# A new order for the first block's products, a narrow idle stream of zeros, and zeroing moved to GpSimd

## The chip, the cores and the metric

The kernel runs on one core of a Trainium2 chip. A core has five engines, each with its own queue of instructions: TensorE (PE in the profile; its weight loads are PEld), VectorE (DVE), ScalarE (ACT), GpSimd (POOL) and SyncE (SP, which here only issues transfers). Engines wait for one another by semaphores, and each engine runs its own instructions in the order in which they were written. The metric is the device time of one execution in microseconds (us); lower is better.

## The reference

Two stages follow each other. The first is a linear attention with decay, for 4 sequences (b), 8 heads (h), 768 steps (t) and 64 elements per head; the second is a feed-forward layer on the 3072 tokens, of width 512 and hidden width 2048.

```python
gamma = 1.0 - 2.0 ** (-5.0 - np.arange(H))
for t in range(S):
    state = gamma[None, :, None, None] * state + np.einsum('bhd,bhe->bhde', k[:, :, t], v[:, :, t])
    y[:, :, t] = scale * np.einsum('bhd,bhde->bhe', q[:, :, t], state)
...
h = np.maximum(x @ w_in, 0.0)          # x: y as 3072 x 512
return h * h @ w_out
```

## The kernel before

**Chunks and blocks.** Each sequence is cut into 6 chunks of 128 steps, 24 chunks in all. Within a chunk the attention is computed with matrices: scores of every key against every query, masked, times the values (`scores`, `outputs`); what earlier chunks contribute goes through a 64 x 64 state per head (`state`). The decay is put into scale factors of q and k (`scale_q`, `scale_kv`). q and k are turned on TensorE (`transpose_q`, `transpose_k`), and ScalarE copies the turned tiles out: `qT` at L414, `k_bd` at L428 in two halves. `outputs` leaves the chunk in a bank that ScalarE copies to `xt` (L531). Chunks 0 to 3 are done in pairs by `..._pair` functions, chunks 4 to 7 by `attend`, and later ones by `attend2`. The feed-forward layer works on blocks of chunks: block 0 has four chunks (512 tokens), the others two.

**The front.** Before the first block there is no feed-forward work. The code loads q, k, v and the first quarter of `w_in` (SP's queue), scales, turns and multiplies for chunks 0 to 3, and between these products it lets TensorE run idle products, `keep_awake(n)` (L359): n products of 128 x 512 with the identity matrix `ident`, whose result nobody reads. `ident` is made by GpSimd (L237, L238). `cast_pair_v` casts the values of a pair to bf16, on GpSimd or with `on_scalar` on ScalarE.

**Block 0.** `ffn_pieces(0)` is a generator; each `yield` ends a piece. Pieces 4 to 15 compute one 128-row slice each of `x @ w_in` (L848) with `relu` (L857) and a squaring on VectorE (L828). Then `second_products` multiplies by `w_out`. Two of its four chunks are done plainly (`plain(j)`, two row blocks of `w_out` each, L1039). The other two are done with seven instead of eight block products, which needs sums and differences of blocks: of `w_out` (`sum_w_out`: `t1` to `t4` in the tiles `w_sum`, L336, on VectorE) and of the hidden values (`s1` to `s4`, L1002, on VectorE). `product(...)` (L1006) multiplies them into four half-bank results `pa`, `pb`, `pd`, `pe`; several of them are started with the first half of the products (`lo`) and ended with the second (`hi`). ScalarE copies the first part of `pa` to `a` (L1063) before further products are added onto `pa`. `w_out` comes in four quarters by `load_w_out(g)` on GpSimd's queue (L185); `plain(2g)` and `plain(2g+1)` use quarter g, the second half of the sums uses quarters 2 and 3.

**The hand-written schedule.** `put(place, what, ...)` puts an action before the piece with that number. Before each piece `before(n)` runs the actions of place n in the order in which they were put, and then the squarings (`take_squares`). So one list of places sets the order of every engine's queue. The numbers for chunk 4 before the change are: `scale_q` at 13 and 15, `scale_kv` at 18, `transpose_q` 19, `transpose_k` 21, `scores` 23 and 25, `state` 25, `outputs` 29; for chunk 5: `scale_kv` 25, `transpose_k` 28, `scores` 30 and 32, `outputs` 34. In block 0 the pieces after place 16 are: `plain(0)` to `plain(3)` (places 16 to 19), first halves of `pd` and `pb` (20), `plain(4)`, `plain(5)` (21, 22), first half of `pe` (23), `plain(6)`, `plain(7)` (24, 25), `pa` (26), `pd` (27), `pb` (28), `pe` (29), and the two halves of `s3` times `t3` onto `pb` (30, 31). Block 1 begins at place 32.

Some tiles that stand beside blocks have off-diagonal halves that must be zero; `zero_off_diagonal` (L375) writes them on VectorE at places 35 to 44.

Of the kernel before, what the change touches and what calls it, by code (L numbers as in the profile page):

```python
# [9 lines left out]
FP32 = mybir.dt.float32  # L10
BF16 = mybir.dt.bfloat16
I32 = mybir.dt.int32

AF = mybir.ActivationFunctionType
ALU = mybir.AluOpType
# [16 lines left out]
def kernel(  # L32
# [9 lines left out]
    nc = tc.nc  # L42
    P = nc.NUM_PARTITIONS
# [152 lines left out]
        load_w_in(g)  # L196


    lng = const.tile([P, H], FP32)
    for h in range(H):  # L200
        nc.gpsimd.memset(lng[:, h : h + 1], float(np.log(gammas[h])))
# [125 lines left out]
    HN = DM // 2  # L327
    sums = [const.tile([P, NFB // 2, HN], BF16, name=f"w_sum{i}") for i in range(4)]

    def sum_w_out(half):  # L330

        src = w_out_halves[half].rearrange("s (j k) (n c) -> s k n j c", k=2, n=2)
        (b11, b12), (b21, b22) = ([src[:, k, n] for n in range(2)] for k in range(2))
        t1, t2, t3, t4 = (t[:, 4 * half : 4 * half + 4] for t in sums)
        for out, in0, in1 in ((t1, b12, b11), (t2, b22, t1), (t3, b22, b12), (t4, b21, t2)):
            yield nc.vector.tensor_tensor(out=out, in0=in0, in1=in1, op=ALU.subtract)  # L336

    def cast_w(kind, g, halves=(0, 1), on="VVSG"):

# [11 lines left out]

    idle_ps = []

    def keep_awake(n, width=4 * C, pool=ps_f, name="psf"):
        if not idle_ps:
            idle_ps.append(pool.tile([P, 4, P], FP32, name=name))
        wide = max(1, width // C)
        for _ in range(n):
            nc.tensor.matmul(  # L359
                idle_ps[0][:, 0:wide, 0 : width // wide],  # L360
                lhsT=ident[:],
                rhs=ident[:, None, 0 : width // wide].to_broadcast([P, wide, width // wide]),
                start=True,
                stop=True,
            )

    def end_awake():
        idle_ps.clear()
# [3 lines left out]
    xts = {}  # L372

    def zero_off_diagonal(t, hh):
        nc.vector.memset(t[halves[hh], :, 1 - hh, :], 0.0)  # L375

    def scale(engine, out, by, table):
        engine.tensor_tensor(  # L378
# [204 lines left out]
    def cast_pair_v(m, r, on_scalar=False):  # L583
        at[m]["v"] = pair_view(v_bd2s[m // 2])
        if on_scalar:
            nc.scalar.activation(at[m]["v"][:, r], raw_v[m][:, r], AF.Copy)
        else:
            nc.gpsimd.tensor_copy(at[m]["v"][:, r], raw_v[m][:, r])
# [392 lines left out]
    def last_of_first():  # L981

        def halves_of(k, c):
            return [
                t.rearrange("e (j k) (c t) -> e k c j t", k=2, c=4)[:, k, 2 + c] for t in h2s[0]
            ]

        (a11, a12), (a21, a22) = ([halves_of(k, c) for k in range(2)] for c in range(2))
        n = NFB // 4
        s1, s2, s4 = (  # L990
            [
                t.rearrange("e (x j t) -> e x j t", x=2, t=C)[:, x]
                for x in range(2)
            ]
            for t in (spare[:, i * HN * 4 : (i + 1) * HN * 4] for i in range(3))
        )
        s3 = a21
        b = lambda k, c: lambda j: w_out_bf[j // 2][:, 2 * (j % 2) + k, c * HN : (c + 1) * HN]
        t1, t2, t3, t4 = (lambda j, t=t: t[:, j] for t in sums)

        def add(out, in0, in1, op=ALU.add):
            nc.vector.tensor_tensor(out=out, in0=in0, in1=in1, op=op)  # L1002

        def product(to, left, right, js, start=True, stop=True):
            for j in js:
                nc.tensor.matmul(  # L1006
                    to,
                    lhsT=left[j // n][:, j % n],
                    rhs=right(j),
                    start=(start and j == 0),  # L1010
                    stop=(stop and j == NFB // 2 - 1),
                    skip_group_check=True,
                )

        def first_sums(x):
            add(s1[x], a21[x], a22[x])
            add(s2[x], s1[x], a11[x], ALU.subtract)

        def last_sums():
            for x in range(2):  # L1020
                add(s3[x], a11[x], a21[x], ALU.subtract)
            for x in range(2):
                add(s4[x], a12[x], s2[x], ALU.subtract)

        def second_products():
            ops = [ps_f.tile([P, DM], FP32, name="psf") for _ in range(2)]
            pa, pe, pd, pb = (
                t[:, n * HN : (n + 1) * HN]
                for t in [ps_f.tile([P, DM], FP32, name="psf") for _ in range(2)]
                for n in range(2)  # L1030
            )
            oa, ob = (opool.tile([P, DM], FP32, name="osb") for _ in range(2))
            a, u, v = (upool.tile([P, HN], FP32, name=f"u{i}") for i in range(3))
            r0 = 2 * C

            def plain(j):
                for f in (2 * j, 2 * j + 1):
                    for c, op in enumerate(ops):
                        nc.tensor.matmul(  # L1039
                            op[:],  # L1040
                            lhsT=h_of(0, f)[:, 0, c * C : (c + 1) * C],
                            rhs=w_out_bf[f // FPQ][:, f % FPQ, :],
                            start=(f == 0),
                            stop=(f == NFB - 1),
                        )
                product(pa, a11, b(0, 0), (j,))

            lo, hi = range(0, 4), range(4, 8)
            for j in range(4):
                plain(j)  # L1050
                yield
            product(pd, s1, t1, lo)
            product(pb, s2, t2, lo, False)
            yield
            for j in range(4, 6):
                plain(j)
                yield
            product(pe, a22, t4, lo, False)
            yield
            plain(6)  # L1060
            yield
            plain(7)
            nc.scalar.activation(a[:], pa, AF.Copy)  # L1063
            for c, op in enumerate(ops):
                osb = opool.tile([P, DM], FP32, name="osb")
                nc.scalar.activation(osb[:], op[:], AF.Copy)
                nc.sync.dma_start(out[c * C : (c + 1) * C], osb[:])
            yield
            product(pa, a12, b(1, 0), lo, False)
            product(pa, a12, b(1, 0), hi, False)  # L1070
            nc.scalar.activation(oa[:, 0:HN], pa, AF.Copy)
            yield
            product(pd, s1, t1, hi)
            yield
            product(pb, s2, t2, hi)
            add(u[:], pb, a[:])
            yield
            product(pe, a22, t4, hi)
            yield
            product(pb, s3, t3, lo, False)  # L1080
            yield
            product(pb, s3, t3, hi, False)
            add(v[:], pb, a[:])
            add(ob[:, HN:DM], pd, v[:])
            add(ob[:, 0:HN], pe, v[:])

            def last_product():
                product(pd, s4, b(1, 1), range(8), False)
                add(oa[:, HN:DM], pd, u[:])
                yield  # L1090
                nc.sync.dma_start(out[r0 + C : r0 + 2 * C], ob[:])
                yield
                nc.sync.dma_start(out[r0 : r0 + C], oa[:])
                yield

            kept.append(last_product())
            yield

        return first_sums, last_sums, second_products

    open_ps = {}

# [15 lines left out]
    def ffn_pieces(tb):  # L1118
        nch = BLOCKS[tb]
        TB = nch * C  # L1120
        if tb == 0:
            first_sums, last_sums, second_products = last_of_first()
            put(11, first_sums, 0)
            put(17, first_sums, 1)
            put(22, last_sums)
            for f in range(FPQ, NFB):
                hp = ps_f.tile([P, TB], FP32, name="psf")
                first_product(tb, hp[:], f, slice(0, TB))
# [70 lines left out]
    def small_pt():  # L1199
        return ptpool.tile([P, NPAIR, 2, C], BF16, name="pt").rearrange("s p hh t -> s (p hh t)")  # L1200

    spare = hpool.tile([P, 4096], BF16, name="h2")
    keep_awake(7, pool=ps_y, name="y")
    scale_q4(0, 0)
    scale_q4(0, 1)
    transpose_q4(0, 0, *tp)
# [39 lines left out]
    state_pair(0, 1, "SV")  # L1246
    cast_w("in", 0, (0,), "GGGG")
    cast_pair_v(2, 0)
    cast_pair_v(2, 1)
    first_unit(0, 0, 0, (0,))  # L1250
    first_unit(0, 0, 1, (0,))
    cast_w("in", 0, (1,), "GGVV")
# [21 lines left out]
    def put(place, what, *args):  # L1274
        parts.setdefault(place, []).append((what, args))
# [4 lines left out]
    def attend(m, scaled, places):  # L1280
        if m % 2 == 0:
            put(scaled, scale_q, m, 0)
            put(scaled + 2 if m == 4 else scaled, scale_q, m, 1)
            put(places[0], transpose_q, m)
        put(18 if m == 4 else places[0], scale_kv, m)
        put(places[1], transpose_k, m)
        put(places[2], scores, m, 0)
        put(places[3], scores, m, 1)
        put(places[3], state, m)
        put(places[4], outputs, m)  # L1290
# [20 lines left out]
    for m, which, place in ((6, "k", 16), (6, "v", 17), (7, "k", 18), (7, "v", 19)):  # L1311
        put(place, load_kv, m, which)
    put(10, cast_w, "in", 3)
    for half, at_places in enumerate(((20, 20, 20, 20), (24, 24, 26, 26))):
        made = sum_w_out(half)
        for place in at_places:
            put(place, next, made)
    attend(4, 13, (19, 21, 23, 25, 29))
    attend(5, None, (25, 28, 30, 32, 34))
    attend(6, 31, (33, 35, 37, 39, 42))  # L1320
    attend(7, None, (38, 42, 44, 46, 49))
    packed = pack_constants()
    put(27, next, packed)
# [76 lines left out]
```

## Time and profile before

| What | Value |
|---|---|
| median of 3 runs | 204.95 us (204.93 to 205.1) |
| the profiled execution's own time | 205.18 us |
| its span in the trace | 203.0 us |
| busy share of the span: PE, PEld, DVE, ACT, POOL | 96%, 80%, 74%, 63%, 37% |
| chain that ended last: share on PE | 93% |
| data read from and written to memory, mean rate | 27.26 MB and 6.29 MB, 165 GB/s |

All times inside the execution are counted from the start of the span. The profiled execution lies 0.23 us above the median, and 2.2 us of it lie outside the span. A busy PE includes the idle products of the front.

### The profile page before, as it was taken

How to read it: one execution, taken by the hardware profiler on the slowest of the kernel's cores; microseconds unless marked ns; L12 is line 12 of the kernel's file. 1: busy time of each engine (PE TensorE's matmuls, PEld its weight loads, DVE VectorE, ACT ScalarE, POOL GpSimd, SP SyncE). 2: the span in 40 equal slices, each digit the busy share in tenths (PEclk: the TensorE clock that was granted, in tenths of full speed). 3: DMA queues.
4: the chain of work that ended last, by engine and by line, in shares of the span. 5: the costliest groups of instructions: out<-in, count | busy, mean ns of one | idle time of the engine just before them, and what ended most of it. 6: DMA issues, size and time to landing. Idle time of an engine off the chain costs nothing.

```text
span 203.0 us, 5812 instructions
## 1 busy us (share of the span) xinstructions
PE 195.8 (96%) x2351; PEld 163.3 (80%) x2351; DVE 150.0 (74%) x322; ACT 127.5 (63%) x258; POOL 75.4 (37%) x143
## 2 busy tenths in 40 slices
PE   5989999999999999999999999999999999999993
PEld 1558545669975998999999999999899999999883
DVE  3786898898797679677787777777787787485374
ACT  8764873455744676693794784774785775763730
POOL 8683721087220873461722084323382022100000
PEclk9999999999999999999999999999999999999999
DMA  5999999999798798979999479999999856200202
GB/s 167 356 374 397 321 198 196 243 232 251 226 203 200 190 141 131 200 180 251 145 215 197 140 130 187 175 227 199 166 133 195 155 107 53 103 3 0 107 0 105
DMA packets 92250, 36.55 MB, mean 180 GB/s; under 512 B 68544, under 2 KB 88256, under 8 KB 92224
## 3 DMA queue, kind: packets, MB, share of 16 engines
q1 hardware_dynamic: 77312, 32.52, 67.8%
q0 software_dynamic: 14912, 3.67, 19.2%
q8 instruction: 18, 0.29, 0.6%
q14 instruction: 8, 0.07, 0.1%
HBM read 27.26 MB, written 6.29 MB: 165 GB/s over the span
## 4 chain that ended last, share of the span: by engine, by line
PE 93%; DVE 2%; DMA 2%; issue 1%; ACT 1%; DVEq 0%
PE psf L848 42%; PE psf L882 18%; PE tp L882 7%; PE psf L1039 3%; PE psf L1174 3%; PE psf L1006 3%; DMA qn<-in_q_dram 2%; PE y L805 2%; PE st L749 2%; PE y L798 2%; PE c_ps L776 2%; PE c_ps L644 1%; PE y L359 1%; PE y L523 1%; PE st L447 1%
## 5 line engine op out<-in xcount | busy, mean ns | idle before, releaser
L848 PE MATMUL psf<-xt,w_in_bf 128*128 128x256 bf16 (+2 forms) x880 | 92.3, 259 | 0.2 <-issue 0.2
L848 PEld LDWEIGHTS <-w_in_bf 128*128 128x128 bf16 x880 | 71.2, 98 | 11.4 <-issue 0.2
L857 ACT ACTIVATE h<-psf 128x512 bf16<-128x512 f32 x96 | 56.1, 595 | 21.3 <-PE psf L848 19.0
L828 DVE TENSOR_TENSOR h<-h 128x512 bf16<-128x512 bf16 x80 | 33.6, 432 | 21.6 <-ACT h L857 21.2
L727 POOL COPY v_bd<-v 64x512 bf16<-64x512 bf16 x32 | 21.6, 675 | 75.0 <-DVE v L719 70.9
L882 PEld LDWEIGHTS <-h 128*128 128x128 bf16 x288 | 26.5, 98 | 3.0 <-DVE h L828 0.3
L160 POOL DMA_DIRECT2D k_big<-in_k_dram x32 | 21.1, 675 | 0.0
L882 PE MATMUL psf<-w_sum,h 128*128 128x256 bf16 x136 | 19.1, 273 | 0.0
L882 PE MATMUL tp<-w_out_bf,h 128*128 128x256 bf16 x136 | 19.1, 273 | 0.0
L882 PE MATMUL psf<-w_sum,k_bd 128*128 128x256 bf16 x144 | 17.9, 273 | 0.0
L878 DVE TENSOR_TENSOR u<-psf,u 128x256 f32<-128x256 f32 x18 | 7.6, 424 | 11.2 <-PE psf L882 10.8
L882 PEld LDWEIGHTS <-k_bd 128*128 128x128 bf16 x144 | 13.8, 98 | 1.5
L785 ACT ACTIVATE s_bd<-c_ps 64x256 bf16<-64x256 f32 x29 | 10.7, 370 | 6.5 <-PE c_ps L776 6.5
L878 DVE TENSOR_TENSOR osb<-psf,u 128x256 f32<-128x256 f32 x26 | 10.3, 421 | 6.1 <-PE psf L882 5.8
L378 DVE TENSOR_TENSOR qs<-qn,qf 128x512 bf16<-128x512 f32 x20 | 14.2, 713 | 0.0
L786 ACT ACTIVATE s_bd<-c_ps 64x256 bf16<-64x256 f32 x29 | 11.0, 379 | 0.4
L756 DVE TENSOR_TENSOR pt<-st,cmask 128x512 bf16<-128x512 f32 x16 | 11.0, 688 | 0.1
L719 DVE TENSOR_TENSOR v<-stage,kf 128x512 bf16<-128x512 f32 x16 | 11.0, 685 | 0.0
L812 ACT ACTIVATE xt<-y 128x512 bf16<-128x512 f32 x16 | 9.6, 599 | 1.8 <-PE y L805 1.2
L918 ACT ACTIVATE osb<-tp 128x256 f32<-128x256 f32 x8 | 3.1, 385 | 12.2 <-PE tp L882 12.2
L826 ACT ACTIVATE h<-h 128x512 bf16<-128x512 bf16 x16 | 10.1, 630 | 0.5
L878 DVE TENSOR_TENSOR k_bd<-h 128x512 bf16<-128x512 bf16 x18 | 10.1, 559 | 0.3
(149 smaller groups left out, 296.1 us busy)
## 6 DMA issues: line engine op xcount, KB each, us to landing
qn<-in_q_dram SPq DMA_DIRECT2D x12, 512.0 KB, 5.5
out_dram<-osb SPq DMA_DIRECT2D x23, 256.0 KB, 2.6
stage<-in_v_dram SPq DMA_DIRECT2D x32, 96.0 KB, 4.1
stage<-in_moe_w_in_dram SPq DMA_DIRECT2D x4, 512.0 KB, 7.2
stage<-in_moe_w_in_dram SPq DMA_DIRECT2D x2, 1024.0 KB, 8.4
w_out_bf<-in_moe_w_out_dram POOLq DMA_DIRECT2D x4, 512.0 KB, 10.1
kn<-in_k_dram SPq DMA_DIRECT2D x6, 256.0 KB, 6.3
k_big<-in_k_dram POOLq DMA_DIRECT2D x32, 48.0 KB, 3.8
```

The costliest lines, as they stand in the source:

```text
L160: nc.gpsimd.dma_start(t[rows, :, p, hh, :], k[b, 2 * p + hh, (i + 3 * n) * C : (i + 3 * n + 3) * C].rearrange("(w s) d -> s w d", s=64),)
L378: engine.tensor_tensor(out=out, in0=by, in1=table[:, :, None].to_broadcast([P, H, D]), op=ALU.mult)
L719: nc.vector.tensor_tensor(out=v2.rearrange("s (u p) d -> s u p d", u=2), in0=vn, in1=kf2[:, i, :, :, None].to_broadcast([P, 2, NPAIR, D]), ...
L727: nc.gpsimd.tensor_copy(v_bd[rows, :, hh, :], v2[rows])
L756: nc.vector.tensor_tensor(out=pt[:], in0=st[:], in1=cmask2.rearrange("s r t -> s (r t)")[:, None, :].to_broadcast([P, 2 * NPAIR, C // 2]), ...
L785: nc.scalar.activation(s_bd[halves[0], :, 0, :], c[halves[0]], AF.Copy)
L786: nc.scalar.activation(s_bd[halves[1], :, 1, :], c[halves[1]], AF.Copy)
L828: nc.vector.tensor_mul(hv, hv, hv)
L848: nc.tensor.matmul(hp, lhsT=w_in_bf[g][:, cb, fq * 128 : (fq + 1) * 128], rhs=xts[tb][:, cb, cols], start=(cb == 0), stop=(cb == NCB - 1),)
L857: nc.scalar.activation(hv, hp[:], AF.Relu)
L878: nc.vector.tensor_tensor(out=out, in0=in0, in1=in1, op=op)
L882: nc.tensor.matmul(to, lhsT=left[:, j], rhs=right(j) if callable(right) else right[:, j], start=(start and j == 0), stop=(stop and j == NF ...
```

## The change

Six edits are made together.

- **Idle products.** The tile `spare` is taken earlier, its last 128 columns (`still`) are zeroed by VectorE as its first instruction, and `keep_awake(n)` now issues 4n products of 128 x 128 with `still` on both sides, instead of n products of 128 x 512 with `ident`. The first call has n = 10 instead of 7.
- **Sums of `w_out`.** The four sums of the first half stay at place 20. Of the second half, `t1` and `t2` are made in two parts, for quarter 2 at place 22 and for quarter 3 at place 24; `t3` and `t4` come whole at place 26. Before, they came at 24, 24, 26 and 26. There are ten instructions instead of eight.
- **Order in block 0 after `plain(7)`.** The second halves of `pd` and `pb` and the addition `u` come first, as one piece (26); then the two halves of `pa` (27, 28); then the two halves of `s3` times `t3` (29, 30); then the second half of `pe` (31). The sums `s3` move from place 22 to 26, and `s4` from 22 to 27.
- **Chunk 4.** `scale_q` comes at 12 and 14, `scale_kv` at 16, `transpose_q` at 17, `transpose_k` 19, `scores` 21 and 23, `state` 23, `outputs` 28. Chunk 6 has its `scale_q` at 30 instead of 31. Chunk 5 keeps its places.
- **A cast.** The second cast of the values of chunks 2 and 3 goes to ScalarE.
- **Zeroing.** `zero_off_diagonal` runs on GpSimd.

```diff
--- before.py
+++ after.py
@@ -195,6 +195,10 @@
     for g in range(2, NQ):
         load_w_in(g)
 
+
+    spare = hpool.tile([P, 4096], BF16, name="h2")
+    still = spare[:, 4096 - P : 4096]
+    nc.vector.memset(still, 0.0)
 
     lng = const.tile([P, H], FP32)
     for h in range(H):
@@ -327,13 +331,14 @@
     HN = DM // 2
     sums = [const.tile([P, NFB // 2, HN], BF16, name=f"w_sum{i}") for i in range(4)]
 
-    def sum_w_out(half):
+    def sum_w_out(half, which=range(4), js=slice(0, 4)):
 
         src = w_out_halves[half].rearrange("s (j k) (n c) -> s k n j c", k=2, n=2)
-        (b11, b12), (b21, b22) = ([src[:, k, n] for n in range(2)] for k in range(2))
-        t1, t2, t3, t4 = (t[:, 4 * half : 4 * half + 4] for t in sums)
-        for out, in0, in1 in ((t1, b12, b11), (t2, b22, t1), (t3, b22, b12), (t4, b21, t2)):
-            yield nc.vector.tensor_tensor(out=out, in0=in0, in1=in1, op=ALU.subtract)
+        (b11, b12), (b21, b22) = ([src[:, k, n, js] for n in range(2)] for k in range(2))
+        t1, t2, t3, t4 = (t[:, 4 * half : 4 * half + 4][:, js] for t in sums)
+        made = ((t1, b12, b11), (t2, b22, t1), (t3, b22, b12), (t4, b21, t2))
+        for out, in0, in1 in (made[n] for n in which):
+            nc.vector.tensor_tensor(out=out, in0=in0, in1=in1, op=ALU.subtract)
 
     def cast_w(kind, g, halves=(0, 1), on="VVSG"):
 
@@ -351,18 +356,11 @@
 
     idle_ps = []
 
-    def keep_awake(n, width=4 * C, pool=ps_f, name="psf"):
+    def keep_awake(n, pool=ps_f, name="psf"):
         if not idle_ps:
-            idle_ps.append(pool.tile([P, 4, P], FP32, name=name))
-        wide = max(1, width // C)
-        for _ in range(n):
-            nc.tensor.matmul(
-                idle_ps[0][:, 0:wide, 0 : width // wide],
-                lhsT=ident[:],
-                rhs=ident[:, None, 0 : width // wide].to_broadcast([P, wide, width // wide]),
-                start=True,
-                stop=True,
-            )
+            idle_ps.append(pool.tile([P, P], FP32, name=name))
+        for _ in range(4 * n):
+            nc.tensor.matmul(idle_ps[0][:], lhsT=still, rhs=still, start=True, stop=True)
 
     def end_awake():
         idle_ps.clear()
@@ -372,7 +370,7 @@
     xts = {}
 
     def zero_off_diagonal(t, hh):
-        nc.vector.memset(t[halves[hh], :, 1 - hh, :], 0.0)
+        nc.gpsimd.memset(t[halves[hh], :, 1 - hh, :], 0.0)
 
     def scale(engine, out, by, table):
         engine.tensor_tensor(
@@ -1016,9 +1014,11 @@
             add(s1[x], a21[x], a22[x])
             add(s2[x], s1[x], a11[x], ALU.subtract)
 
-        def last_sums():
+        def third_sums():
             for x in range(2):
                 add(s3[x], a11[x], a21[x], ALU.subtract)
+
+        def fourth_sums():
             for x in range(2):
                 add(s4[x], a12[x], s2[x], ALU.subtract)
 
@@ -1066,22 +1066,22 @@
                 nc.scalar.activation(osb[:], op[:], AF.Copy)
                 nc.sync.dma_start(out[c * C : (c + 1) * C], osb[:])
             yield
+            product(pd, s1, t1, hi)
+            product(pb, s2, t2, hi)
+            add(u[:], pb, a[:])
+            yield
             product(pa, a12, b(1, 0), lo, False)
+            yield
             product(pa, a12, b(1, 0), hi, False)
             nc.scalar.activation(oa[:, 0:HN], pa, AF.Copy)
-            yield
-            product(pd, s1, t1, hi)
-            yield
-            product(pb, s2, t2, hi)
-            add(u[:], pb, a[:])
-            yield
-            product(pe, a22, t4, hi)
             yield
             product(pb, s3, t3, lo, False)
             yield
             product(pb, s3, t3, hi, False)
             add(v[:], pb, a[:])
             add(ob[:, HN:DM], pd, v[:])
+            yield
+            product(pe, a22, t4, hi)
             add(ob[:, 0:HN], pe, v[:])
 
             def last_product():
@@ -1096,7 +1096,7 @@
             kept.append(last_product())
             yield
 
-        return first_sums, last_sums, second_products
+        return first_sums, (third_sums, fourth_sums), second_products
 
     open_ps = {}
 
@@ -1122,7 +1122,8 @@
             first_sums, last_sums, second_products = last_of_first()
             put(11, first_sums, 0)
             put(17, first_sums, 1)
-            put(22, last_sums)
+            put(26, last_sums[0])
+            put(27, last_sums[1])
             for f in range(FPQ, NFB):
                 hp = ps_f.tile([P, TB], FP32, name="psf")
                 first_product(tb, hp[:], f, slice(0, TB))
@@ -1199,8 +1200,7 @@
     def small_pt():
         return ptpool.tile([P, NPAIR, 2, C], BF16, name="pt").rearrange("s p hh t -> s (p hh t)")
 
-    spare = hpool.tile([P, 4096], BF16, name="h2")
-    keep_awake(7, pool=ps_y, name="y")
+    keep_awake(10, pool=ps_y, name="y")
     scale_q4(0, 0)
     scale_q4(0, 1)
     transpose_q4(0, 0, *tp)
@@ -1246,7 +1246,7 @@
     state_pair(0, 1, "SV")
     cast_w("in", 0, (0,), "GGGG")
     cast_pair_v(2, 0)
-    cast_pair_v(2, 1)
+    cast_pair_v(2, 1, on_scalar=True)
     first_unit(0, 0, 0, (0,))
     first_unit(0, 0, 1, (0,))
     cast_w("in", 0, (1,), "GGVV")
@@ -1282,7 +1282,7 @@
             put(scaled, scale_q, m, 0)
             put(scaled + 2 if m == 4 else scaled, scale_q, m, 1)
             put(places[0], transpose_q, m)
-        put(18 if m == 4 else places[0], scale_kv, m)
+        put(16 if m == 4 else places[0], scale_kv, m)
         put(places[1], transpose_k, m)
         put(places[2], scores, m, 0)
         put(places[3], scores, m, 1)
@@ -1311,13 +1311,13 @@
     for m, which, place in ((6, "k", 16), (6, "v", 17), (7, "k", 18), (7, "v", 19)):
         put(place, load_kv, m, which)
     put(10, cast_w, "in", 3)
-    for half, at_places in enumerate(((20, 20, 20, 20), (24, 24, 26, 26))):
-        made = sum_w_out(half)
-        for place in at_places:
-            put(place, next, made)
-    attend(4, 13, (19, 21, 23, 25, 29))
+    put(20, sum_w_out, 0)
+    put(22, sum_w_out, 1, (0, 1), slice(0, 2))
+    put(24, sum_w_out, 1, (0, 1), slice(2, 4))
+    put(26, sum_w_out, 1, (2, 3))
+    attend(4, 12, (17, 19, 21, 23, 28))
     attend(5, None, (25, 28, 30, 32, 34))
-    attend(6, 31, (33, 35, 37, 39, 42))
+    attend(6, 30, (33, 35, 37, 39, 42))
     attend(7, None, (38, 42, 44, 46, 49))
     packed = pack_constants()
     put(27, next, packed)
```

## The prediction

> **What bounds the kernel now.** I read the head of the page first, then its chain of work that ended last.
>
> ```profile
> span 203.0 us, 5812 instructions
> PE 195.8 (96%) x2351; PEld 163.3 (80%) x2351; DVE 150.0 (74%) x322; ACT 127.5 (63%) x258; POOL 75.4 (37%) x143
> ...
> PE 93%; DVE 2%; DMA 2%; issue 1%; ACT 1%; DVEq 0%
> ```
>
> TensorE is the bound nearly everywhere. A change that leaves its products as they are can only move two things: how late the dense stream of products begins, and the holes in it. So the second view is that of the waits of PE alone, all of it:
>
> ```profile
> PE y L359 <- POOL ident L238: 2.2, 1, 2.2
> PE c_ps L601 <- DVE ks_bdp L576: 0.9, 1, 0.9
> PE psf L1006 <- ACT u L1063: 0.5, 1, 0.5
> PE psf L848 <- issue: 0.2, 1, 0.2
> ```
>
> Two holes belong to the front (before 18 us), one to block 0. Third, the timeline of the front, start and length in us, to see how fast PE runs and what its hole at 10.76 hangs on:
>
> ```profile
> 7.33 1.01 PE L359 MATMUL y<-ident 128*128 128x512 bf16 x2
> 8.17 0.39 PE L567 MATMUL psf<-ident,qs 128*128 128x128 bf16 x4
> 9.01 0.69 DVE L625 TENSOR_TENSOR pt<-st,maskp 128x512 bf16<-128x512 f32 x1 [0.98 <-PE psf L617]
> 9.12 1.04 POOL L576 TENSOR_TENSOR ks_bdp<-kn,kfp 128x512 bf16<-128x512 f32 x1 [0.18 <-DMA kn<-in_k_dram]
> 9.62 1.08 DVE L576 TENSOR_TENSOR ks_bdp<-kn,kfp 128x512 bf16<-128x512 f32 x1
> ...
> 12.33 0.60 PE L359 MATMUL y<-ident 128*128 128x512 bf16 x2
> ```
>
> The same pair of idle products takes 1.01 us at 7.33 and 0.60 us at 12.33. Four turns took 0.61 us at 5.47 and 0.39 us at 8.17. So PE runs at half speed until about 8.2 us, 6.0 us after its first product at 2.19. VectorE's mask at 9.01 waited 0.98 us for slow products; its next step, the scaling of k for chunks 2 and 3, began at 9.62 although the k it reads had landed by 9.1 (GpSimd's wait for the same transfer ended at 9.12). Fourth, the timeline around the end of block 0's products:
>
> ```profile
> 39.56 0.60 PE L1006 MATMUL psf<-w_sum,h 128*128 128x256 bf16 x4
> 40.14 1.02 PE L1039 MATMUL psf<-w_out_bf,h 128*128 128x512 bf16 x4
> ...
> 42.42 0.27 PE L1006 MATMUL psf<-w_out_bf,h 128*128 128x256 bf16 x1
> 42.73 0.39 ACT L1063 ACTIVATE u<-psf 128x256 f32<-128x256 f32 x1 [0.60 <-PE psf L1006]
> 43.17 1.03 PE L1006 MATMUL psf<-w_out_bf,h 128*128 128x256 bf16 x8 [0.47 <-ACT u L1063]
> 44.48 0.39 PE L421 MATMUL tp<-ident,ks 128*128 128x128 bf16 x4
> 44.90 1.21 ACT L428 ACTIVATE k_bd<-tp 64x512 bf16<-64x512 bf16 x2 [0.28 <-PE tp L421]
> 46.13 0.60 ACT L531 ACTIVATE xt<-y 128x512 bf16<-128x512 f32 x1
> ```
>
> Products follow each other at 0.22 us (512 columns), 0.11 (256) and 0.056 (128), read from neighbouring starts. So PE stood idle from 40.00 to 40.14 and from 42.53 to 43.17. The second hole is ScalarE's copy of `pa` to `a`. The first is a transfer: the view of the tile `w_out_bf` has its four issues from 22.6 to 25.8 and landings after 6.7 to 14.3 us; the last issue with the longest landing gives 40.1, and `plain(6)` is the first user of that quarter.
>
> **The change, part by part.** I sum against the profiled execution, 205.18 us (span 203.0 and 2.2 outside it); the median, 204.95, is 0.23 lower, and I carry the difference over. From block 1 on PE has no hole above 0.2 us, so what is gained or lost by the start of block 1 (47.63) arrives at the end.
>
> *Order after `plain(7)`.* Eight products of 256 columns (0.87 us) now stand between the end of `plain(7)` and the first that overwrites what `a` is copied from. The copy needs 0.64. The hole goes: **−0.64**. This holds if `t1` and `t2` are ready. VectorE after place 23, at its own steps: mask 0.61, state copy 0.41, two half-size sums 0.67. With 0.39 more, which a sum lost at 41.08 beside GpSimd's cast (1.07 against 0.68), they end at about 41.5; PE asks at 42.1. The next in VectorE's queue are `scale_kv(5)`, `t3`, `t4`, `s3` and `u`, done at about 44.4; PE asks for them at 44.7. No wait, with 0.3 us to spare; without that cover up to 0.4.
>
> *Chunk 4 sooner.* The products are the same, in other places. Ahead of `plain(6)` now stand the second scores and the state of chunk 4, 8 products or 0.45 us, which fill the 0.14 before the landing: **−0.14**. Both need the mask of the first scores (VectorE about 38.0, PE at 39.1) and the values cast by GpSimd (row 34.59), in time. But `outputs(4)` moves from 29 to 28, ahead of `transpose_k(5)`, and fewer products follow that turn. Count from the start T of `outputs(4)`. PE: outputs 0.67, turn 0.22, half of `pa` 0.44, half of `s3` 0.44, so it asks for `scores(5, 0)` at T+1.77. ScalarE runs in order: first the copy to `xt`, from T+0.87 (0.20 after the last product, as from 44.70 to 44.90), step 0.55; then the two copies of `k_bd`, 1.21, to T+2.63, and 0.06 for the signal. PE waits **+0.92**. Before, 1.55 us of products lay after the turn and the copies stood ahead of `xt`, so there was no wait. Bounds: 0.59 if `xt` did not stand in the way, 1.1 with full durations and a slower start. I take 0.92, since each row is of the same instruction. Behind the waiting scores stand the other half of `s3`, `pe` and block 1.
>
> *Idle products and the cast.* VectorE's zeroing can start with the other engines at 0.75, by the row of L375 for 0.17; so idle products start at about 1.0 instead of 2.19. Forty at 0.107 end by 5.3, before q has been scaled (5.4). If full speed again takes 6.0 us, it comes at 7.0. The turn of k (6.90), its copy (7.57) and the scores (8.49) then come up to 0.7 earlier, the mask ends by 9.1, and the scaling of k starts when its transfer lands, 9.1 instead of 9.62. That 0.5 runs through masks, state and `xt` to the first L848 at 15.23. The cast that moves to ScalarE lies there at about 15.25 to 15.85, where PE wants it at about 15.85: 0 to 0.15 lost. I take **−0.40**. Bounds: 0 (full speed no earlier) and −0.75 (k landing sooner, and the 0.24 of "issue" at 17.99 falling elsewhere: 57 more products and as many weight loads shift where that stall lies). The waits of `w_in` are unchanged; GpSimd's casts end their waits with the landings.
>
> *What the front runs into.* `plain(6)` would be asked for at 40.00 + 0.45 − 0.40 = 40.05; the quarter of `w_out` lands at 40.1, issued behind GpSimd's cast of the third quarter of `w_in`, which waits for its own transfer (L346, 21.42), so it doesn't move with the front. **+0.09**; a larger front gain would be lost here.
>
> *Off the path.* Two more sums, 0.06. `s3`, `s4` later: `s4` is used in block 1. Zeroing: ten memsets of 0.17 to 0.27 leave VectorE between 53 and 62 us; GpSimd gets them at up to 0.52 (its row for 64x512), 5 us where it is busy two tenths. Queued behind them are its casts of k (52.20 and 55.78), its transfer to `k_big` at 56.34 and SP's turning transfer that waits for the casts; 0.7 later at most, first used by the scores at 70.88. VectorE's mask took 0.69 during GpSimd's long memsets (43.49 to 49.1), so memsets beside it cost nothing. SP's loads keep their places.
>
> Sum: −0.64 − 0.14 + 0.92 − 0.40 + 0.09 = −0.17, or 205.01 in the profiled execution and **204.8** as median.
>
> The Trainium skill, "TensorE: Matmul & The Clock Gate", Part 1, has half speed end after one busy window of about 3.4 us that runs free of the kernel's start, so the lead lies between 3.4 and 6.8 us. The 6.0 us seen agrees. By this rule full speed comes between 4.4 and 7.8 us, the front gains between 0.2 and 0.4, and the sum lies between −0.17 and −0.06 as an estimate.
>
> **The rivals.** What a measurement can tell from no change is about 0.2%, 0.41 us.
>
> *Faster: a larger front, a smaller wait.* The front gains 0.75, the wait before `scores(5, 0)` is 0.59, and the quarter of `w_out` lands 0.2 sooner because the execution that is timed carries no profile. −0.64 − 0.14 + 0.59 − 0.75 + 0.24 = −0.70: 204.25. For it: ScalarE's copies overlap by some 0.1 in the rows, and the median lies 0.23 under the profiled execution. Against: all have to fall well.
>
> *Slower: idle products that don't count.* Zeros of 128 columns, each with a weight load, may keep PE less active than the 512-column products did; then half speed holds until the real products are dense. If it lasts past 9.5 us, it decides: PE's work between 8.2 and 11.6 is some 2.4 us at full speed, the slack there 1.0, so the front loses about 0.6. −0.64 − 0.14 + 0.92 + 0.60 = +0.74: 205.7.
>
> *Slower: VectorE late.* With a front that gains nothing, the sum is +0.14; if `u` (0.3 to spare) is late by 0.4 more, `s3`'s products wait: +0.5, 205.45.
>
> *Nothing moves.* The two removed holes and the new one cancel and the front is set by transfers: +0.14; it lies inside the forecast.
>
> **How the numbers follow.** Forecast with the last case 0.43 (within 0.2%); the faster rival 0.36, since both its ends, the front and the wait, have wide bounds to that side; the idle products 0.11; VectorE 0.10. So faster 0.36, same 0.43, slower 0.21. The forecast's own range is 204.55 to 205.1. The whole range takes in the faster rival and part of the slower ones: 204.0 to 205.5.
>
> **What would show it.** Idle products from about 1.0; four turns at 0.39 instead of 0.61 at latest by 7 us; VectorE's L576 at 9.1; first L848 at 14.8. No wait on L1063. A new wait of PE on ScalarE's `k_bd` (L428) of 0.9 us in block 0. I am wrong if that wait is missing or under 0.5, if full speed comes after 8.2, or if PE waits for the sums of `w_out`.

## The result, and the profile after

The changed kernel takes **204.01 us** (median of 22 executions, 203.70 to 204.82), the kernel before 204.77 beside it (22 executions, 204.20 to 205.76). The ratio is **0.9965**, with a 95% interval from 0.9955 to 0.9975: faster by 0.35%, 0.7 to 0.8 us. The spreads of the two overlap, and a part of that spread has a cause that the experiments show below. The profiled executions lie further apart, 203.70 against 205.18, with spans of 201.9 and 203.0. So 1.04 us of their distance lies in the spans, and 0.44 outside them: an execution's time less its span is 2.2 us before and 1.8 after (zero_cast, below, says which edit does that).

The head of the page after, and all of PE's waits:

```profile
span 201.9 us, 5925 instructions
PE 196.4 (97%) x2403; PEld 167.2 (83%) x2408; DVE 148.5 (74%) x315; ACT 127.8 (63%) x259; POOL 81.1 (40%) x152
...
PE 94%; DVE 2%; ACT 1%; issue 1%; DVEq 0%
```

```profile
PE y L363 <- DVE h L201: 1.0, 1, 1.0
PE st L445 <- ACT k_bd L426: 0.3, 1, 0.3
PE psf L1004 <- DVE u L1000: 0.2, 1, 0.2
PE psf L599 <- POOL ks_bdp L574: 0.2, 1, 0.2
PE c_ps L599 <- DVE ks_bdp L574: 0.2, 1, 0.2
PE psf L1175 <- issue: 0.2, 1, 0.2
```

The wait on ScalarE's copy to `a` (0.5) is gone, and so are the long wait on the scaled k (0.9) and the "issue" at 17.99. In their place stand two new ones in block 0: on `u` (VectorE) and on `k_bd` (ScalarE). The timeline of the front after, start and length in us:

```profile
1.00 4.45 PE L363 MATMUL y<-h 128*128 128x128 bf16 x40 [1.00 <-DVE h L201]
5.45 0.61 PE L565 MATMUL tp<-ident,qs 128*128 128x128 bf16 x4
6.05 0.40 PE L565 MATMUL st<-ident,qs 128*128 128x128 bf16 x4
7.67 2.95 POOL L574 TENSOR_TENSOR ks_bdp<-kn,kfp 128x512 bf16<-128x512 f32 x2 [1.51 <-DMA kn<-in_k_dram]
8.32 0.69 DVE L623 TENSOR_TENSOR pt<-st,maskp 128x512 bf16<-128x512 f32 x1 [0.31 <-PE psf L615]
9.02 0.69 DVE L574 TENSOR_TENSOR ks_bdp<-kn,kfp 128x512 bf16<-128x512 f32 x1
...
14.26 1.07 PE L846 MATMUL psf<-xt,w_in_bf 128*128 128x128 bf16 x16
14.64 0.61 POOL L586 CAST v_bd<-vn 128x512 bf16<-128x512 f32 x1 [1.31 <-DMA vn<-in_v_dram]
```

Two rows of PE in the kernel before, to compare with:

```profile
15.23 1.07 PE L848 MATMUL psf<-xt,w_in_bf 128*128 128x128 bf16 x16
17.99 1.05 PE L848 MATMUL psf<-xt,w_in_bf 128*128 128x128 bf16 x16 [0.24 <-issue]
```

Four turns take 0.61 at 5.45 and 0.40 at 6.05: full speed came at 5.9 us (before: 8.15). The mask and the scaling of k come 0.7 and 0.6 earlier, and the scaling takes 0.69 instead of 1.08. The first L846 (L848 before) stands at 14.26 instead of 15.23. The cast of v at 14.64, in the view after, is bad news: the second half of v landed at 14.58, where it had landed at 13.41 before. Block 0 after:

```profile
43.31 0.39 PE L419 MATMUL tp<-ident,ks 128*128 128x128 bf16 x4
43.51 0.60 ACT L529 ACTIVATE xt<-y 128x512 bf16<-128x512 f32 x1 [0.62 <-PE y L521]
43.86 0.42 DVE L1000 TENSOR_TENSOR u<-psf,u 128x256 f32<-128x256 f32 x1
44.00 1.20 ACT L426 ACTIVATE k_bd<-tp 64x512 bf16<-64x512 bf16 x2
44.34 0.60 PE L1004 MATMUL psf<-w_sum,h 128*128 128x256 bf16 x4 [0.21 <-DVE u L1000]
44.77 0.22 PE L445 MATMUL st<-qT,k_bd 128*128 128x128 bf16 x1
45.25 0.34 PE L445 MATMUL st<-qT,k_bd 128*128 128x128 bf16 x3 [0.26 <-ACT k_bd L426]
```

ScalarE copies `xt` first and `k_bd` after it, as forecast; PE stands 0.37 us before 44.34 and 0.42 before 45.25 (from the start of the product before, less its 0.11 or 0.06 us).

Where the time went, by three marks on PE: the first 512-column product of block 0 came at 20.53 (before 21.59), block 1 began at 46.59 (before 47.63), the span ends 1.04 earlier. Between the first two marks lie 26.04 us before and 26.06 after. So all of the difference between the two spans is the front's, and block 0 is even: 0.64 and 0.14 us of holes removed, 0.37 and 0.42 made. For the medians this does not hold: beside the experiments the median span of the kernel before is 202.6, that of the changed kernel is 202.2, so about 0.4 of the 0.76 us lies in the span and about 0.4 outside it.

### The profile page after: what moved, and what is told of

Its sections match the earlier page's. It is cut to its first block, busy times and chain, and to the rows that moved or that the text cites. A ratio compares the mean times of both kernels' runs of the same rounds, so it can differ in the third digit from the quotient of the medians.

```text
span 201.9 us, 5925 instructions
## 1 busy us (share of the span) xinstructions
PE 196.4 (97%) x2403; PEld 167.2 (83%) x2408; DVE 148.5 (74%) x315; ACT 127.8 (63%) x259; POOL 81.1 (40%) x152
## 4 chain that ended last, share of the span: by engine, by line
PE 94%; DVE 2%; ACT 1%; issue 1%; DVEq 0%
PE psf L846 42%; PE psf L880 18%; PE tp L880 7%; PE psf L1175 3%; PE psf L1039 3%; PE y L363 3%; PE psf L1004 3%; PE st L747 2%; PE y L803 2%; PE y L796 2%; PE c_ps L774 2%; PE c_ps L642 1%; PE st L445 1%; PE y L521 1%; DVE osb L876 1%
## 5 line engine op out<-in xcount | busy, mean ns | idle before, releaser
L846 PE MATMUL psf<-xt,w_in_bf 128*128 128x256 bf16 (+2 forms) x879 | 92.3, 259 | 0.1
L846 PEld LDWEIGHTS <-w_in_bf 128*128 128x128 bf16 x880 | 71.2, 98 | 11.2
```

Of the source, the lines that this page charges most:

```text
L846: nc.tensor.matmul(hp, lhsT=w_in_bf[g][:, cb, fq * 128 : (fq + 1) * 128], rhs=xts[tb][:, cb, cols], start=(cb == 0), stop=(cb == NCB - 1),)
```

## The experiments

Two theories stood against each other: A, the gain is the front's; B, it is block 0's. "Under the kernel before" means the kernel before on the same chip in the same session (medians 204.84 to 204.86).

**front_only.** The kernel before with the new idle stream alone:

```diff
+    spare = hpool.tile([P, 4096], BF16, name="h2")   # ahead of the constants
+    still = spare[:, 4096 - P : 4096]
+    nc.vector.memset(still, 0.0)
...
-    keep_awake(7, pool=ps_y, name="y")     # 128x512 with ident
+    keep_awake(10, pool=ps_y, name="y")    # 4n of 128x128 with still
```

> The kernel before with the new idle stream alone (zeros of 128 columns, 40 of them first, started by VectorE's memset). Theory A, the gain is the front's: in the changed kernel the first L848 came at 14.26 instead of 15.23 us, so up to 0.97 us; of it the wait for the last quarter of w_out before plain(6) takes back 0.1 to 0.4 here, since that quarter lands with GpSimd's issue and not with TensorE. Expected 0.5 to 0.9 us under the kernel before, with the first L848 near 14.3. Theory B, the gain is block 0's: plain(6) waits for the transfer and eats the front's gain, so within 0.2 us of the kernel before.

Measured: 204.34, ratio 0.9978 (0.9967 to 0.9989), so 0.45 under the kernel before, a little less than expected by A, more than B allows. All of it lies in the span (202.1 against 202.6). The first L844 came at 14.30. But the products that read v waited for GpSimd's two casts:

```profile
14.84 1.17 POOL L584 CAST v_bd<-vn 128x512 bf16<-128x512 f32 x2 [1.49 <-DMA vn<-in_v_dram]
15.50 0.14 PEld L664 LDWEIGHTS <-v_bd 64*64 64x64 bf16 x8 [0.31 <-POOL v_bd L584]
16.06 0.37 PEld L664 LDWEIGHTS <-v_bd 64*64 64x64 bf16 x24 [0.41 <-POOL v_bd L584]
```

These are the timeline's rows: two stops, 0.30 and 0.41 us of PE, that neither kernel had. Of the 0.93 gained by the first L844, 0.45 was left at the first 512-column product (21.14). From there to block 1 the old order took 25.90 us, 0.16 less than the new one (26.06): the last quarter of `w_out` landed at 39.34, so of the two old holes only the larger was left. By these marks the new order of block 0 doesn't pay beside an early front; no run has the new front and the cast with the old order.

**block_only.** The kernel before with the new order in block 0, places and parts of the sums; front, cast and zeroing as before (the part of the diff from `sum_w_out` on, without those two lines).

> The kernel before with the new order in block 0 alone (places of chunks 4 and 6, parts of the sums, order of the products); front, cast and zeroing as before. Theory A: two holes of 0.64 and 0.14 us go, new waits of 0.8 us for u and for k_bd come (in the changed kernel 0.37 and 0.42), so within 0.2 us of the kernel before. Theory B: 0.4 us or more under it.

Measured: 204.51, ratio 0.9994 (0.9980 to 1.0008). No difference that can be told, as A has it. The time alone only just excludes B's 0.4 us, which is the end of the interval; what speaks against B is the profile, where block 0 is even (0.78 us of holes removed, 0.79 made). The holes are those of the changed kernel: 0.37 before `s3`, 0.42 inside `scores(5, 0)`. This profile held a surprise. Its front is that of the kernel before, but its first L849 stands at 14.24, as early as in the changed kernel; its clock had come up at 6.54.

**zero_cast.** The kernel before with `nc.gpsimd.memset` in `zero_off_diagonal` and `cast_pair_v(2, 1, on_scalar=True)` alone.

> The kernel before with the zeroing on GpSimd and the one cast on ScalarE alone. Both theories: within 0.2 us of the kernel before. A rival, that VectorE freed of ten memsets gains later: 0.2 to 0.4 us under it.

Measured: 204.71, ratio 0.9997 (0.9987 to 1.0007): nothing in the whole. But two parts cancel in it. Outside the span its 12 executions have 1.72 to 1.81 us, those of the kernel before beside it 2.17 to 2.29. The three kernels with the zeroing on VectorE (before, block_only, front_only) all have about 2.2, and all with it on GpSimd about 1.8 (first_narrow 2.0, with two executions of 2.6 and more), cast_back too, so it is the zeroing and not the cast. The profiles of those three show a packet of instructions (8 KB) that begins 1.0 to 1.2 us after the span's end; of the other ten only first_narrow's shows one there (16 KB), in an execution with 2.6 us outside. That this packet is the 0.4 us is inferred from this, not shown. Inside, its median span is 202.95, longer by 0.35: none of its 12 executions has a span under 202.6, where 11 of 29 of the kernel before have one. Why is open.

**cast_back.** The changed kernel with `cast_pair_v(2, 1)` on GpSimd again.

> The changed kernel with the second cast of the values of chunks 2 and 3 back on GpSimd. If the later landing of v makes that cast late (front_only alone: holes of 0.30 and 0.41 us before the products that read it), it is 0.4 to 0.7 us slower than the changed kernel, 0.1 to 0.4 under the kernel before. If the cast is as free as it was alone (zero_cast), within 0.15 us of the changed kernel.

Measured: 204.26, ratio 0.9975 (0.9964 to 0.9986), 0.24 over the changed kernel, less than expected; in its profile the stop is 0.41 us and the first 512-column product comes at 20.91 instead of 20.53. So the cast showed no gain without the new front (zero_cast) and is worth about a quarter to 0.4 us beside the new idle stream, because that stream made v late.

**narrow_late.** The changed kernel with `still` made from `ident` (VectorE, after GpSimd has made it) and `keep_awake(7)` first.

> The changed kernel with its zeros made from the identity matrix by VectorE, so that the narrow idle products start at about 2.3 instead of 1.0 us, and with 28 instead of 40 of them first. Theory A (what counts is when TensorE gets its full clock, and that comes one to two windows of 3.4 us after the first product): full clock up to 1.3 us later, so that a good part of the executions misses the point, between 6.8 and 7.8 us, from which the front ends 0.9 us later; median 0.2 to 0.6 us above the changed kernel. If the width of the products is what helps: within 0.15 us of the changed kernel.

Measured: 204.59, ratio 0.9989 (0.9977 to 1.0001), 0.58 over the changed kernel. What it has under the kernel before, 0.26, is less than the 0.4 outside the span; its median span is 202.8 against 202.6. The idle products began at 3.08, later than I had meant; the clock rose at 8.12, and the first L846 stood at 15.23 again. Eleven of its 12 executions lie between 204.55 and 204.72, one at 203.82, as if that one had caught an early clock. Narrow products are no help when they start late.

**wide_early.** The changed kernel with its zeros in 512-column products:

```diff
-        for _ in range(4 * n):
-            nc.tensor.matmul(idle_ps[0][:], lhsT=still, rhs=still, start=True, stop=True)
+        for _ in range(n):
+            nc.tensor.matmul(idle_ps[0][:], lhsT=still,
+                             rhs=still[:, None, :].to_broadcast([P, 4, P]), start=True, stop=True)
```

> The changed kernel with its zeros in products of 128 x 512 (10 first, a quarter as many instructions), started as early as in the changed kernel. Theory A1, only the start counts: the same time within 0.15 us, first L848 near 14.3. Theory A2, the narrow products cost something too: TensorE has 54 products and as many weight loads more to fetch, and a 16 KB packet of instructions that moved 15.57 us in the kernel before moved at 11.9 to 12.2 in the three kernels with narrow products, where the second half of v landed at 14.6 to 14.8 instead of 13.4. Then the packet comes after 14 us here, that half of v lands at 13.4 again, and the time is the same or up to 0.2 us lower. Theory A3, zeros or wide products don't raise the clock: 0.4 us or more slower.

Measured: 204.40, ratio 0.9981 (0.9972 to 0.9991), about 0.4 over the changed kernel. None of the three had this: A3 had the size, but not the reason. The packet (16 KB of instructions) came at 14.69 and v landed at 13.37, as A2 said, the clock rose at 6.25, and the first L852 stood at 14.24. What was lost is a stop of PE that waited for nothing that the profile shows:

```profile
16.22 0.45 PE L648 MATMUL c_ps<-v_bd,ks_bdp 64*128 64x128 bf16 x5
16.96 0.32 PE L648 MATMUL c_ps<-v_bd,ks_bdp 64*128 64x128 bf16 x3 [0.29 <-issue]
```

It parts eight equal products in the middle. In the kernel before the stop of the same kind (17.99) lay ahead of an L848 product. Counted along PE's queue, weight loads and products together, it is the 450th instruction in both.

**turn_first.** The changed kernel with the two lines of `attend` for chunks 5 and 4 exchanged, so that at place 28 `transpose_k(5)` comes before `outputs(4)`.

> The changed kernel with transpose_k(5) ahead of outputs(4) at place 28, so that ScalarE copies k_bd before xt. If TensorE's stop of 0.42 us inside scores(5, 0) is ScalarE's queue, it goes and the time falls by 0.3 to 0.5 us against the changed kernel, about 1.1 us under the kernel before. If the hole only moves (to the wait for u, or into block 1), within 0.15 us of the changed kernel, 0.6 to 0.9 under the kernel before.

Measured: 204.02, ratio 0.9963 (0.9949 to 0.9976), the changed kernel's time: the second case. The 0.42 us went, block 1 began at 46.18 instead of 46.59, and then `scores(6, 0)` stood 0.69 us for ScalarE's next `k_bd`:

```profile
51.73 0.24 ACT L300 ACTIVATE kf<-ex_k_f 128x48 f32<-128x48 f32 x1 [0.98 <-DVE ex_k_f L215]
51.88 0.58 ACT L855 ACTIVATE h<-psf 128x512 bf16<-128x512 f32 x1
52.36 1.20 ACT L426 ACTIVATE k_bd<-tp 64x512 bf16<-64x512 bf16 x2
```

ScalarE's small exponential from `pack_constants` waits for VectorE, and behind it the copies of `k_bd` are late.

**best.** wide_early with turn_first's exchange, `t4` of the second half moved from place 26 to 28, and `put(34, next, packed)` moved to 39.

> The changed kernel with wide zeros, transpose_k(5) ahead of outputs(4), the fourth sum of the second half of w_out at place 28 instead of 26 (so that u comes 0.6 us sooner on VectorE), and the second step of pack_constants at 39 instead of 34 (in turn_first ScalarE waited 0.98 us for VectorE there, ahead of the copies of k_bd of chunk 6, and TensorE stood 0.69 us). If these are the three holes that are left (0.37, 0.42, and what turn_first brought), all go: 0.6 to 0.9 us under the changed kernel. If a hole only moves again, 0.1 to 0.5 under it.

Measured: 204.38, ratio 0.9982 (0.9971 to 0.9994): 0.36 over the changed kernel, so the expectation failed. It had wide_early's stop at 16.97. The holes of block 0 went (block 1 at 46.30), and a new pair of 0.47 and 0.56 us came in `scores(7, 0)` at 61: the exponential, now at place 39, waited 3.35 us for VectorE and held up the copies of chunk 7.

**first_narrow.** wide_early with only the first idle call in 40 narrow products.

> wide_early with its first idle call alone in narrow products (40 of 128 columns); the later calls stay wide. That gives TensorE 60 instructions more than wide_early and 50 fewer than the changed kernel. Theory of instruction supply: in five kernels with wide idle products TensorE stood 0.36 to 0.49 us before its 450th instruction, whichever that was, some 2.3 us after a 16 KB packet of instructions had begun to move (14.6 to 15.6 us). Here the packet begins near 13.0, is there by 15.3, and the 450th instruction comes at about 15.5 or later: no such hole, and the time is 0.3 to 0.5 us under wide_early, that of the changed kernel. If the width of the later idle products matters instead, it stays with wide_early (0.4 us over the changed kernel).

Measured: 204.63, ratio 1.0000 (0.9988 to 1.0013): the expectation failed. But the packet did not begin at 13.0, it began at 13.65, and PE stood 0.43 us before 15.95, in yet another line:

```profile
PE st L676 <- issue: 0.2, 1, 0.2
```

It is the 450th instruction again, 2.3 us after the packet's start. So the rule held (which instruction, and when it can run), and my time for the packet was wrong.

**after_again.** The changed kernel once more.

> The changed kernel once more, as the base for the two beside it: 0.6 to 0.9 us under the kernel before. Its profile: if full clock comes before 7 us, the first L848 is at 14.2 to 14.3; if after 7.5, at 15.2, and the execution is 0.6 to 0.9 us longer.

Measured: 204.02, ratio 0.9968 (0.9957 to 0.9980); clock at 4.32, first L846 at 14.23.

**best2.** The changed kernel, narrow zeros kept, with the exchange, `t4` at 28, and the second step of `pack_constants` behind all copies of `k_bd`:

```diff
-    put(26, sum_w_out, 1, (2, 3))
-    attend(4, 12, (17, 19, 21, 23, 28))
+    put(26, sum_w_out, 1, (2,))
+    put(28, sum_w_out, 1, (3,))
     attend(5, None, (25, 28, 30, 32, 34))
+    attend(4, 12, (17, 19, 21, 23, 28))
...
-    put(34, next, packed)
+    put(46, next, packed)
```

> The changed kernel with transpose_k(5) ahead of outputs(4), the fourth sum at 28 instead of 26, and the second step of pack_constants at 46 instead of 34 (behind the copies of k_bd of chunks 6 and 7; at 34 and at 39 ScalarE waited there for VectorE and these copies came late, with 0.69 and 1.03 us of holes). The narrow zeros stay, so that the hole of instruction supply stays away. If all three holes go: 0.6 to 0.8 us under the changed kernel. If ScalarE's next queue makes a new hole in block 1 again: 0.0 to 0.3 us under it.

Measured: **203.00**, ratio 0.9924 (0.9906 to 0.9941), 1.02 under after_again. These rows in its timeline, where the changed kernel had its two stops, follow each other without one:

```profile
43.52 0.60 PE L1004 MATMUL psf<-w_out_bf,h 128*128 128x256 bf16 x4
43.96 0.60 PE L1004 MATMUL psf<-w_sum,h 128*128 128x256 bf16 x4
44.39 0.39 PE L445 MATMUL st<-qT,k_bd 128*128 128x128 bf16 x4
```

A stop of 0.15 us is left at 45.21. Block 1 begins at 45.86 (46.56 in after_again, a gain of 0.70), and no new stop on ScalarE follows; after_again's own 0.16 in `scores(6, 0)` and 0.20 at 59.05 are gone too. The end of PE's work moves from 198.93 to 197.94, the same 1.0.

**All profiles side by side.** The time of full clock is from the trace's clock record; the packet is the first 16 KB of instructions inside the span; "v" is the landing of its second half, "w" that of the second half of the first quarter of `w_in`; "450th" is the start of PE's 450th instruction, all in us.

| Kernel | full clock | first `x @ w_in` product | packet | v, w | 450th | stop there |
|---|---|---|---|---|---|---|
| before | 8.15 | 15.23 | 15.57 | 13.41, 14.76 | 17.99 | 0.40 |
| zero_cast | 7.77 | 15.17 | 15.62 | 13.37, 14.72 | 17.99 | 0.38 |
| narrow_late | 8.12 | 15.23 | 12.83 | 13.39, 15.95 | 16.08 | none |
| block_only | 6.54 | 14.24 | 14.72 | 13.38, 14.73 | 16.96 | 0.36 |
| wide_early | 6.25 | 14.24 | 14.69 | 13.37, 14.72 | 16.96 | 0.45 |
| best | 4.17 | 14.21 | 14.63 | 13.34, 14.71 | 16.97 | 0.49 |
| first_narrow | 6.30 | 14.26 | 13.65 | 13.42, 16.16 | 15.95 | 0.43 |
| after | 5.94 | 14.26 | 11.92 | 14.58, 15.88 | 14.44 | none |
| after_again | 4.32 | 14.23 | 11.88 | 14.56, 15.85 | 14.40 | none |
| front_only | 5.30 | 14.30 | 12.21 | 14.79, 16.08 | 14.48 | none |
| cast_back | 6.48 | 14.27 | 12.06 | 14.56, 15.86 | 14.45 | none |
| turn_first | 6.79 | 14.28 | 12.12 | 14.62, 15.91 | 14.46 | none |
| best2 | 4.21 | 14.25 | 11.94 | 14.55, 15.85 | 14.43 | none |

Three things stand in it. First, the front has two outcomes in these profiles: with full clock by 6.8 us it ends at 14.2 to 14.3, from 7.8 on at 15.2; no profile lies between. Second, the stop of about 0.4 us belongs to a place in PE's queue, not to a line. Third, where the packet of instructions begins before 14 us, the landing due next is 1.2 to 1.4 us later (v, or the half of `w_in`); where it begins after 14.6, neither is.

## Why the prediction was right or wrong

The range held the time by 0.01 us (204.01, lower end 204.0), which is luck; the likeliest case (within 0.2%, 204.8, with a range of its own from 204.55) did not come. What came is the size of the faster rival (0.70 under, 0.76 measured), and two of its three reasons: a front that gains more, and an earlier landing of `w_out` (in the profile too, so not for the reason given). The agreement in size is in part luck as well. About 0.4 of the 0.76 us lies outside the span and comes with the zeroing. The prediction had these "2.2 outside it" as a constant and put the zeroing off the path, at no cost and no gain; that step failed. What the rival summed, inside the span, moved the median by 0.4 only.

**Front: the mechanism was right, the size was not.** Forecast 0.40, measured 0.97 at the first product and 1.06 at the first 512-column product. Idle products from 1.00, and the scaling of k at 9.02, were as told. What I left out is the length of that scaling: before, GpSimd's scaling had begun at 9.12 and VectorE's, begun at 9.62, took 1.08; now VectorE begins first and takes 0.69, and GpSimd's is the one that is drawn out (from the start of its first to the end of its second 2.95, before 2.47; in block_only the second alone took 1.55, before 1.04). That is the 0.39 between my 14.8 and the measured 14.26, with some 0.15 besides. It also goes with the two outcomes: in the ten profiles with the early front VectorE's scaling begins at 8.99 to 9.06 and takes 0.69, in the three with the late one it begins at 9.41 to 9.82 and takes 0.87 to 1.23. Who reads first is decided by whether the mask is done by 9.0. The Trainium skill, "SBUF — State Buffer", section "SBUF: two separate sides", calls the port pair that the two engines share an exclusive lock, taken by whichever begins first against a VectorE operation with two SBUF inputs; these rows agree in who pays, 0.39 and 0.51 us.

**Clock.** I took 6.0 us from the first product to full speed from the one profile. The thirteen profiles have 3.2 to 6.0; the two of 3.2 (best, best2) lie just under the 3.4 that I had as the least. That the record of full clock lasts 194.56 or 197.97 us in every profile, 57 or 58 times 3.413, agrees with the free-running window of "TensorE: Matmul & The Clock Gate" in the Trainium skill, Part 1. The estimate that I drew from it (front 0.2 to 0.4) was too low for the same missing 0.39.

**Profile and median.** I carried the 0.23 between the profiled execution and the median over as a constant. It is not one: that profile had the late front, and the kernel before has executions of both kinds, as block_only's profile with the same front shows. So the profiles differ by 1.48 and the medians by 0.76, of which about 0.4 lies outside the span in both. The early start seems to make the early outcome the usual one, and the gain inside the span to lie in that: 26 of 30 executions of the changed kernel have spans of 202.4 or less, 30 of 83 of the kernel before beside the experiments, 1 of 12 of narrow_late. Which front an execution had shows only in a profile, so this is a hint and not a count.

**The "issue" at 17.99.** I had it as an end of a range (0.24 falling elsewhere). It did fall elsewhere, for a reason: the runs point to a late supply of instructions (all profiles side by side, above). With narrow products PE comes to its 450th instruction when the packet is there.

**The cast.** Forecast 0 to 0.15 lost; PE did stop 0.14 us at 15.30. That it saves more than that, since the same packet delays v, I did not see.

**Block 0.** Forecast −0.64 and −0.14 removed: both went. The 0.14 can't be laid to the earlier chunk 4, though: front_only, with the old places, has no such hole either. Forecast +0.92 for `k_bd`: measured 0.79, but 0.37 of it stands before `s3`, for `u`. The wait for `k_bd` itself is 0.42, and under 0.5 was one of my signs of being wrong. My margin of 0.3 us there was wrong: `t3`, `t4` and `s3` ended at 43.83 on VectorE, `u` at 44.28, and PE asked at 43.97. VectorE was about as late as I had it (44.4); PE came 0.7 sooner, since the front gained more. In narrow_late, with the late front, PE did not stand for `u`, and the whole wait was for `k_bd`, 0.70. Where `u` is late, the wait for `k_bd` is only the rest. The net of block 0 was forecast as +0.14, and measured as +0.02.

**What the front runs into.** Forecast +0.09, since the last quarter of `w_out` would land at 40.1. It landed at 39.19 and nobody waited. The step "it doesn't move with the front" failed, but the front is not the whole reason: narrow_late, with a late front, has 39.38. Before and zero_cast have 40.1 and 40.2, all others 39.1 to 39.5. Why is open.

**Off the path.** Zeroing and sums at no cost on PE's path: right by the profiles (from the first 512-column product to PE's last, zero_cast takes 178.0 us like the kernel before, block_only too), though zero_cast's longer median span is open. That the zeroing would take 0.4 us off the time outside the span I did not see.

**The slower rivals.** Zeros in narrow products raised the clock in every profile. VectorE was late for `u`, by 0.37, but the wait for `k_bd` behind it took that in.

## What to carry to other kernels

A profile is one execution: where a front races against a clock that rises at its own time, look at the spread of the times and at several profiles before a difference of under 1 us is laid to an edit. When a hole is removed from an engine's stream, find what is next in the queue that would have been late anyway; here a hole closed at one of ScalarE's copies opened at the next (`turn_first`, `best`), and the gain came when the places were cleared together (best2, another 1.0 us). Idle or helper instructions are not free even on an idle engine: they move the transfers of instructions, and these move the data. And keep the span and the time outside it apart: an edit that shows nothing in the whole may have moved both (zero_cast).

## What the runs showed of the hardware that I had not expected

- Instructions come in packets of 16 KB while the data is loaded. In the six kernels that stood there, PE ran its 450th instruction 2.2 to 2.4 us after the start of the first such packet in the span, and had stood 0.36 to 0.49 us before it. The other seven ran it 2.3 us or more after the packet's start, without a stop. The Trainium skill, "Runtime: NRT & Kernel Launch", section "Instruction fetch mechanics", says that each engine's sequencer fetches 16 KiB pages ahead over its own DMA queue and that the cost is mostly hidden; the size agrees with the packets here, the hiding seems to fail in these six profiles. That the packet is PE's and the one with the 450th instruction is inferred from the constant distance, not shown.
- One such packet (0.95 us on its engine) went with a landing 1.2 to 1.4 us later: v from 13.4 to 14.6 or 14.8, or, when the packet came between 12.8 and 13.7, `w_in` from 14.7 to 16.0 or 16.2.
- The clock of TensorE came up between 3.2 and 6.0 us after its first product, and not by the program alone: two executions of the changed kernel, after and after_again, have 4.9 and 3.3.
